# A fixed order for every engine, and the second projection of batches 3 and 4 with still weights, in an attention kernel with a gated long convolution

## The chip, the cores and the metric

The kernel runs on one core of a Trainium2 chip. A core has five engines that run side by side: TensorE (PE) multiplies matrices into PSUM, VectorE (DVE) and ScalarE (ACT) compute on SBUF and PSUM, GpSimd (POOL) computes on SBUF, and SyncE (SP) issues transfers. Sixteen DMA engines move the data that SP, ACT and POOL ask for. Each engine works through its own list of instructions in order and waits on semaphores for the others.

The metric is the time of one execution on the device in microseconds. Before the change it was 381.19 us, the median of three runs (380.57 to 384.06).

## What is computed

Attention over 8 batches, 12 heads, 448 positions, head width 64, with one more term in the denominator, and then a gated convolution over the positions, with the heads joined to a width of 768:

```python
scores = scale * np.matmul(q, k.transpose(0, 1, 3, 2))
m = np.max(scores, axis=-1, keepdims=True)
e = np.exp(scores - m)
attn = e / (np.sum(e, axis=-1, keepdims=True) + np.exp(-m) + 1e-09)
x = np.matmul(attn, v)                       # then (B, S, H * D)
proj = x @ w_proj                            # (768, 2304): x1, x2, x3
X2 = np.fft.rfft(x2, n=S, axis=1)
H = np.fft.rfft(filter_fft, n=S, axis=0)[None, :, :]
x2_conv = np.fft.irfft(X2 * H, n=S, axis=1)
y = x1 * x2_conv * x3
out = y @ w_out
```

Inputs and output are float32; the matrix products are done in bfloat16.

## The kernel before

**Attention.** The work goes by pairs of heads, 6 to a batch, 48 in all; pair i is of batch i // 6. For a pair, the scores are made transposed in four parts: part 0 (lines 825, a remainder of the keys of both heads) and parts 1 to 3 (line 823, 128 keys of each head). ACT takes the exponential of each part (lines 842 and 836). The value products follow, with the remainder first (lines 854 and 862); a column of ones beside v gives the sum. DVE adds 1, takes the reciprocal and multiplies (`norm`, lines 875 to 877). The result `xb` is turned to `xT`, with the channels on the partitions: in batch 0 by PE (line 959), later by DMA transposes on SP (line 950), two for each batch.

**Loads.** In batches 0 and 1 (`staged`) k, q and v come from HBM in float32 (lines 448 and 453, remainders line 465), POOL casts them (lines 475, 481 and 488; for pair 0 it is DVE), and PE turns k and q (lines 514, 516 and 523). From batch 2 on (`loaded`) POOL casts into a buffer `nat` (lines 603, 619, 640, 652), and SP issues DMA transposes into qT and kT (lines 584 and 591), one pair at a time in batch 2 and three pairs at a time later. Weights and the filter come by POOL (lines 717 to 721, 801 and 806).

**The convolution** (`dense`) goes by batch. DVE folds xT into four blocks `xf` by symmetry (lines 1020 to 1028). The second projection, of x2, follows in one of two forms:

- `P` (line 1051): xf is the still operand, the weights move through. 8 groups (4 blocks x 2 halves of the channels) of 6 matmuls of 384 columns. The result has the positions on the partitions, as the next step wants it.
- `PS` (line 1073): the weights are still, xf moves through. 6 groups of 6 matmuls of 452 columns. The result has the channels on the partitions; ACT and DVE copy it in turn into `x2s` (lines 1086 and 1084), and after each three of the six groups SP turns that half with a DMA transpose into `x2` (line 1090).

`TURNED = (5, 6, 7)` names the batches with `PS`. After it come the spectrum (`Z`, lines 1121 and 1125), the products with the filter's spectrum on DVE, the inverse (`I`, line 1210), the unfolding on DVE, and the gates (`G`, line 1171; dt 0 to 5, part 0 and 1, copies at lines 1183 and 1186). Gated y goes through the output projection (`O`, line 987; ACT copies it, line 1285; SP stores it, line 1292). Some of the last projections, all their copies and their stores stand behind a branch (line 1497) that recomputes everything with a maximum where a denominator is too small; with these inputs the branch isn't taken.

**What sets the order.** Each step is added to a planner (`Plan.add`) with its engine, a cost, a wish time, the tokens that it needs and makes, and what it takes and gives back of PSUM banks and buffers. `Plan.run` then goes through time by these costs. At each moment it starts on every free engine the first task, by wish time and among the next 160, that is ready in the plan, and the order in which it started them is the order in which the instructions are written. The planner has a model of the two DMA queues of SP and POOL (delay, landing, shares), gives out PSUM banks (8; score pairs and value products take two each, `hy` tasks, up to five at a time, one each), and from 3 to 36 us fills gaps of PE with small matmuls on a zero tile (line 1438), which keep PE busy. The head starts with 38 such matmuls (`spin`, line 1446). On the chip each engine keeps the written order, and semaphores alone hold it back.

Of the kernel before, what the change touches and what calls it, by code (L numbers as in the profile page):

```python
# [15 lines left out]
BF16 = mybir.dt.bfloat16  # L16
# [4 lines left out]
SP = 112  # L21
NST = S // SP
# [19 lines left out]
class Plan:  # L42
# [11 lines left out]
    LANDING = 1.6  # L54
    DELAY = (1.15, 1.9)
    TURN_ISSUE, TURN_HOLD = 1.4, 0.4
    SHIFT = {}
    OPEN = 8
# [16 lines left out]
    def add(self, eng, cost, want, emit, need=(), make=(), take=(), give=(), dma=0.0, run=256, n=1, after=0.0, begun=(), late=0.0, turn=False, part=None, keep=False, port=False):  # L75
        want += self.SHIFT.get(part, 0.0)
        self.tasks.append((want, len(self.tasks), eng, cost, emit, need, make, take, give, dma, after, run, n, begun, late, turn, keep, port or eng == "POOL" and not dma))

    def run(self):
# [36 lines left out]

        def release():
            h = queues["SP"][0] if queues["SP"] else None
            if h and h[2][1] in begin and h[0] <= clock + 1e-9:
                free["SP"] = max(clock + self.TURN_HOLD, begin.pop(h[2][1]) + self.TURN_ISSUE)  # L120
                heapq.heappush(events, free["SP"])

        def transfers(to):
            nonlocal clock
            while clock < to:
# [7 lines left out]
                step = min([h[1] * total / h[2][11] for h in heads.values()] + [x - clock for x in soon] + [to - clock])  # L133
                clock += step
# [8 lines left out]
        def soonest():  # L143
            heads = [q[0] for q in queues.values() if q and q[0][0] <= clock + 1e-9]
            soon = [q[0][0] for q in queues.values() if q and q[0][0] > clock + 1e-9]
            total = sum(h[2][11] for h in heads)
            return max(min([clock + h[1] * total / h[2][11] for h in heads] + soon), now + 1e-6)
# [25 lines left out]
        def ready(t):  # L173
            e = t[2]
            if t[10] > now + 1e-9:
                return False
# [23 lines left out]
        while any(queue.values()):  # L200
            moved = False
            for e in queue:
                if free[e] > now + 1e-9:
                    continue
                for i, t in enumerate(queue[e][: self.WINDOW]):
# [24 lines left out]
                if t[9]:  # L230
                    q = queues["POOL" if e == "POOL" else "SP"]
                    if t[15]:

                        begin[t[1]], free[e] = now, 1e9
                    q.append([now + self.DELAY[e == "POOL"], t[9], t])
# [54 lines left out]
def kernel(  # L290
# [16 lines left out]
    TURNED = (5, 6, 7)  # L307
# [25 lines left out]
    ld = ctx.enter_context(tc.tile_pool(name="ld", bufs=2))  # L333
# [38 lines left out]
    x2s = nat[:, 0:KNAT].rearrange("p (t a n) -> p t a n", t=NDT, a=4)  # L372
    qn = nat[0:SP, KNAT : 2 * KNAT].rearrange("p (g t c) -> p g t c", g=NHP, t=NST)
# [4 lines left out]
    def stage(g, at, n):  # L378
# [7 lines left out]
            "x2": 1, "x2s": 1, "xs": 2, "t0": 2, "t1": 2, "yh": 1, "g": 1, "x1": 2, "cr": 2, "cw": 1, "cv": 2, "yT": 1, "yR": 1,  # L386
            "os": 3,
        }
    )
    add = plan.add  # L390
# [41 lines left out]
    def staged(b):  # L432
# [3 lines left out]
        for hp in range(NHP):  # L436
# [6 lines left out]
            for n, (name, x, at, size) in enumerate(parts):  # L443
                src = stage(g, at, size)

                def load(name=name, x=x, src=src, hp=hp, g=g):
# [14 lines left out]
                    make=[("s" + name, g)], after=hold, dma=0.92 if name == "q" else 0.7, run=57,  # L461
                    begun=[("i" + name, g)])
                if hp == 0 and name != "q":
# [3 lines left out]
                        dma=1.05, run=57, begun=[("ir", b)])  # L467
# [4 lines left out]
                def cast(name=name, src=src, hp=hp, g=g, eng=eng):  # L472
                    if name == "k":
                        T[g]["kn"] = t = ld.tile([128, 3, 128], BF16, name="k0")
                        eng.tensor_copy(
                            t[:].rearrange("p j (u d) -> p u j d", u=2),
                            src.rearrange("p (u j d) -> p u j d", u=2, j=3),
                        )
                    elif name == "q":
                        T[g]["qn"] = t = ld.tile([SP, NST, 2, DH], BF16, name="q0")  # L480
                        eng.tensor_copy(
                            t[:].rearrange("p j u d -> p u j d"),
# [16 lines left out]
            if hp == 0:  # L499
                for u in range(2):  # L500
# [5 lines left out]
                        need=[("rk", b), "zero ks"] + ([("T", NHP * b - 1)] if b else []), make=[("crk", b)])  # L506
# [68 lines left out]
    def loaded(b):  # L575
# [4 lines left out]
        last = ("S", i0 - NHP - 1, 3)  # L580
# [15 lines left out]

        for n, (name, x) in enumerate((("k", k), ("v", v))):
            add("SP", 0.5, tau(i0) - lead[0] - 0.2 + 0.1 * n,
                lambda name=name, x=x: nc.sync.dma_start(rests[:, "kv".index(name)], shared(x, b)),
                need=[("cr" + name, b - 1)], make=[("r" + name, b)], dma=1.05, run=57)  # L600
        for u in range(2):
# [4 lines left out]
            need=[("rv", b), ("V", i0 - NHP - 1, 1)], make=[("crv", b), ("vr", b)])  # L606

        for hp in range(NHP):
# [8 lines left out]
                need=[("cq", g - QS)] if n >= QS else staged_done, make=[("sq", g)], dma=0.92, run=57)  # L617
# [6 lines left out]
            if hp % few == 0:  # L624
                gs = range(g, g + few)
                add("SP", 1.3, tau(g) - lead[6], lambda hp=hp: q_turn(hp), need=[("cq", i) for i in gs] + [last],
                    make=[("qT", i) for i in gs], dma=(0.65, 1.85)[few > 1], run=11, late=-0.37, turn=few > 1)
            for n, (name, x) in enumerate((("k", k), ("v", v))):
# [3 lines left out]
                room = [("c" + "kv"[old % 2], NHP * NSTAGED + old // 2)] if old >= 0 else staged_done + [  # L632
                    ("T", i) for i in range(NHP * NSTAGED - NHP, NHP * NSTAGED)]
                add("SP", 0.5, tau(g) - lead[0] + 0.1 * n,
                    lambda x=x, hp=hp, src=src: nc.sync.dma_start(src.rearrange("p (u c) -> p u c", u=2), rows(x, b, hp)),
                    need=room, make=[("s" + name, g)], dma=0.7, run=57)
                sv = src.rearrange("p (u j d) -> p u j d", u=2, j=3)
                if name == "k":
# [5 lines left out]
                    if hp % few == 0:  # L644
                        gs = range(g, g + few)
                        add("SP", 1.3, tau(g) - lead[2], lambda hp=hp: k_turn(hp), need=[("ck", i) for i in gs] + [("crk", b), last],
                            make=[("kT", i) for i in gs], dma=(0.95, 1.85)[few > 1], run=11, late=-0.37, turn=few > 1)
                else:
# [5 lines left out]
                    add("POOL", 0.62, tau(g) - lead[3], cast, need=[("sv", g), ("V", g - 2 * NHP, 1)], make=[("cv", g), ("v", g)])  # L654
# [68 lines left out]
    def more_tables():  # L723
# [26 lines left out]
        add("DVE", 1.2, WT, weights, need=["row"], make=["half"], after=WT)  # L750
        add("DVE", 0.35, FT, after=FT, emit=lambda: nc.vector.tensor_scalar(
# [5 lines left out]
        add("DVE", 0.7, BPS, turn_back, need=["bps", "half"], make=["bt"], give=[("hy", "bps")])  # L757
# [3 lines left out]
    def filter_spectrum():  # L761

        def half(par):
            F = W["F"]
            if par == 0:
# [45 lines left out]
    def attention(i):  # L811
# [85 lines left out]
        for t in range(4):  # L897
# [26 lines left out]
            add("ACT", 0.81 if t else 0.44, w - 1.0, lambda t=t: exps(t), need=[("S", i, t)],  # L924
# [624 lines left out]
```

## Time and profile before

| what | value |
|---|---|
| median of three runs | 381.19 us (380.57 to 384.06) |
| the profiled execution's own time | 384.65 us |
| its span, from the first to the last instruction | 382.9 us |
| mean granted TensorE clock | 0.996 |
| PE busy | 365.7 us |
| DVE, ACT, POOL busy | 264.2, 263.5, 109.9 us |
| dummy matmuls in gaps (line 1438), and at the start (line 1446) | 8.8 us, 4.0 us |
| moved by DMA | 66.84 MB, 175 GB/s over the span |

The profile is of one execution, and its durations are those of that execution. In a list of groups, "x576 | 121.8, 352" says that 576 instructions were busy for 121.8 us together and that one took 352 ns on the average. Matmuls overlap in the array, so the durations of single ones add up to more than the busy time; the pace of a run of them is what counts. Idle time of an engine is put down to what ended it, as in "<-DMA qT<-nat". In a list of stretches, DMA is the mean busy share of the 16 engines; their packets overlap, so that it can pass 1.

### The profile page before, as it was taken

Reading aid. Unit: us, or ns where it says so; the run is one execution under the profiler, and the core shown is the slowest. Engines: PE = TensorE matmul, PEld = TensorE weight load, DVE = VectorE, ACT = ScalarE, POOL = GpSimd, SP = SyncE. Lnnn points to the kernel's source line nnn. Section 1 sums busy time; section 2 is a strip of 40 time slices with the busy share of each in tenths; the row PEclk is TensorE's granted clock in tenths of the full one; section 3 lists DMA queues with packets and bytes.
Section 4 is the critical chain, followed back from the end, with each engine's and each line's share of the span. In section 5 each row is a group of like instructions: output and inputs, shape, how many; then the busy total and the mean of one; then the engine's idle time right before and its main releaser. Section 6 shows DMA issues by size and latency. Waiting matters only on the chain. (4 is left out here: it accounts for less than half of the span.)

```text
span 382.9 us, 9530 instructions
## 1 busy us (share of the span) xinstructions
PE 365.7 (96%) x3675; PEld 225.7 (59%) x3675; DVE 264.2 (69%) x677; ACT 263.5 (69%) x457; POOL 109.9 (29%) x240
## 2 busy tenths in 40 slices
PE   8879999999897999999999899999999999999985
PEld 7656666556554576556755565655555556555642
DVE  6377778765799739974499786656586767648650
ACT  5759886776777577777787268887779775444713
POOL 5682716050565242652463443110000000000000
PEclk9989999999999999999999999999999999999999
DMA  8999999996999899999999962493524062323304
GB/s 210 250 231 248 253 220 201 149 225 191 237 251 252 206 242 190 298 233 303 216 230 228 263 181 64 122 192 91 93 35 123 32 121 46 135 64 63 127 4 165
DMA packets 125747, 66.84 MB, mean 175 GB/s; under 512 B 82493, under 2 KB 122112, under 8 KB 125696
## 3 DMA queue, kind: packets, MB, share of 16 engines
q1 hardware_dynamic: 120976, 60.54, 68.2%
q0 software_dynamic: 4480, 5.41, 8.4%
q8 instruction: 29, 0.48, 0.6%
q10 hardware_dynamic: 240, 0.23, 0.2%
q14 instruction: 22, 0.18, 0.1%
HBM read 43.86 MB, written 11.01 MB: 143 GB/s over the span
## 5 line engine op out<-in xcount | busy, mean ns | idle before, releaser
L836 ACT ACTIVATE e<-psum 128x896 bf16<-128x896 f32 x144 | 126.9, 921 | 25.6 <-PE psum L823 25.0
L1171 PE MATMUL psum<-xT,wproj_bf 128*128 128x448 bf16 x576 | 121.8, 352 | 1.7 <-DMA xT<-xb 0.9
L1171 PEld LDWEIGHTS <-wproj_bf 128*128 128x128 bf16 x576 | 54.0, 97 | 47.6 <-issue 4.3
L987 PE MATMUL psum<-wout_bf,yT 128*128 128x384 bf16 x288 | 52.6, 326 | 1.7 <-DVEq L1497 1.7
L1183 ACT CAST x<-psum 128x448 bf16<-128x448 f32 x48 | 25.7, 536 | 28.9 <-PE psum L1171 28.6
L823 PE MATMUL psum<-qT,kT 64*128 64x448 bf16 x288 | 42.4, 358 | 2.9 <-DVE xb L877 2.3
L862 PE MATMUL psum<-vn,e 128*128 128x65 bf16 x1152 | 44.5, 194 | 0.0
L1051 PE MATMUL psum<-wproj_bf,xf 128*113 128x384 bf16 x240 | 43.7, 327 | 0.2
L862 PEld LDWEIGHTS <-e 128*128 128x128 bf16 x1152 | 39.8, 98 | 3.0
L1285 ACT COPY osb<-psum 128x384 f32<-128x384 f32 x56 | 26.4, 488 | 22.1 <-PE psum L987 16.4
L619 POOL CAST nat<-nat 112x512 bf16<-112x512 f32 x36 | 23.8, 666 | 55.0 <-DMA nat<-in_q_dram 51.7
L987 PEld LDWEIGHTS <-yT 128*128 128x128 bf16 x288 | 26.9, 98 | 19.6 <-DVEq L1497 2.0
L1139 DVE TENSOR_TENSOR t<-xs,hrs 113x768 bf16<-113x768 bf16 (+1 forms) x64 | 35.7, 590 | 3.9 <-ACT xs L1133 3.9
L1186 DVE TENSOR_TENSOR g<-x,psum 128x448 bf16<-128x448 bf16 x48 | 29.5, 615 | 11.1 <-PE psum L1171 10.9
L1051 PEld LDWEIGHTS <-xf 128*113 128x113 bf16 x240 | 30.9, 132 | 8.3 <-issue 1.5
L877 DVE TENSOR_TENSOR xb<-psum,den 128x512 bf16<-128x512 f32 x48 | 33.2, 692 | 1.7
L842 ACT ACTIVATE er<-psum 128x448 bf16<-128x448 f32 x48 | 26.5, 552 | 7.6 <-PE psum L825 7.6
L1133 ACT CAST xs<-psum 113x384 bf16<-113x384 f32 (+1 forms) x64 | 28.0, 497 | 4.6 <-PE psum L1121 2.4
L875 DVE TENSOR_SCALAR den<-psum 128x8 f32<-128x8 f32 x48 | 7.8, 162 | 33.2 <-PE psum L862 33.2
L652 POOL CAST vn<-nat 128x192 bf16<-128x192 f32 x58 | 22.5, 414 | 26.5 <-DMA nat<-in_v_dram 15.7
L1219 ACT CAST cr<-psum 128x452 bf16<-128x452 f32 x48 | 25.0, 550 | 5.1 <-PE psum L1210 3.9
L823 PEld LDWEIGHTS <-kT 64*128 64x128 bf16 x288 | 9.4, 94 | 27.7 <-issue 26.3
(125 smaller groups left out, 476.4 us busy)
## 6 DMA issues: line engine op xcount, KB each, us to landing
nat<-in_q_dram SPq DMA_DIRECT2D x47, 224.0 KB, 4.6
out_dram<-osb SPq DMA_DIRECT2D x24, 384.0 KB, 3.3
nat<-in_k_dram SPq DMA_DIRECT2D x41, 192.0 KB, 4.5
nat<-in_v_dram SPq DMA_DIRECT2D x41, 192.0 KB, 4.4
wproj_bf<-in_moe_w_proj_dram POOLq DMA_DIRECT2D x2, 1152.0 KB, 12.8
rests<-in_k_dram SPq DMA_DIRECT2D x8, 192.0 KB, 4.7
rests<-in_v_dram SPq DMA_DIRECT2D x8, 192.0 KB, 4.4
out_dram<-osb SPq DMA_DIRECT2D x8, 192.0 KB, 3.4
```

Source lines behind the costliest of these rows:

```text
L823: nc.tensor.matmul(sc[:, u, 0:S], kT[b % 2][c, hp, t, :], qT[b % 2][c, hp, :])
L836: nc.scalar.activation(to, of, AF.Exp, scale=SCALE)
L842: nc.scalar.activation(to, of, AF.Exp, scale=SCALE)
L862: nc.tensor.matmul(out_bank(u)[:, n, :], P["e"][1 + t][:, u * S + n * 128 : u * S + n * 128 + 128], vn[b % 2][:, hp, 4 * u + t, :], start= ...
L877: nc.vector.tensor_tensor(W["xb", b][:, hp].rearrange("p n (u d) -> p u n d", u=2), op[:, :, :, 0:DH], rec[:].unsqueeze(3).to_broadcast([1 ...
L987: nc.tensor.matmul(ops[:n, :DCH], y[:, dt, 0:n], wout_bf[:, dt, ch * DCH : (ch + 1) * DCH], start=(dt == 0), stop=(dt == NDT - 1),)
L1051: nc.tensor.matmul(pps[:FQ, :DCH], W["xf", b][:, pg, kt, 0:FQ], wproj_bf[:, kt, D + ch * DCH : D + (ch + 1) * DCH], start=(kt == 0), stop= ...
L1133: nc.scalar.copy(L["xs", par, ch][:K, pg % 2, :], L["Z", pg, ch][:K, :DCH])
L1139: nc.vector.tensor_tensor(t[:K], L["xs", par, ch][:K], h, op=ALU.mult)
L1171: nc.tensor.matmul(p[:, :S], wproj_bf[:, kt, 2 * part * D + dt * 128 : 2 * part * D + (dt + 1) * 128], xT()[:, kt, 0:S], start=(kt == 0), ...
L1186: nc.vector.tensor_tensor(g[:, dt, :], L["x1", dt], p[:, :S], op=ALU.mult)
L1285: nc.scalar.copy(L["os", st][:n, ch * DCH : (ch + 1) * DCH], L["O", st, ch][:n, :DCH])
```

## The change

1. **Order.** A tuple `ORDER` gives each of the 2,023 tasks, in the order of `add`, a rank of its own in place of its wish time. With it the planner looks at the first task of each engine's queue only, and no longer at the time before which a task may not start. The plan's run in time still places PSUM banks and dummy matmuls.
2. **The planner's numbers.** Landing, delays and many costs are other ones. A DMA transpose now holds SP in the plan until the transposes ahead of it in the queue are done but for 0.9 us; before, until it came to the front of the queue. All transposes hold SP in this way now. Some needs are written out that the order had given before; the first loads of batch 2 need fewer casts.
3. **Second projection.** `TURNED` takes in batches 3 and 4. Batches 5 to 7 (`WHOLE`) keep their buffer, which lies where k's staging was. Batches 3 and 4 use `x2h`, half as large, so that the second half of the channels waits until the first is turned. It shares its memory with the two-slot buffers of k0 and q0 of batches 0 and 1, which were a tile pool and are now slices of one tile. A memset on DVE clears the part of it that isn't written.

In the new order the engines begin like this (T: turn of a pair; S i,t: scores of pair i, part t; V: value products; ER: remainder of the value products):

- PE: turn of q0, turn of the tables, the 38 dummy matmuls, turn of k0, turn of the k rests, S 0,0, S 0,1, T 1, S 0,2, S 0,3, S 1,1, T 2, S 1,2 with ER 0, ... S 2,3, V 1, S 3,0, S 2,0, T 4, S 3,1, S 3,2 with ER 2, ...
- SP: v2, q1, k rests, v3, k0, k1, v0, v rests, q2, k2, k4, q3, v1, k3, q4, q5, k5, k6, k rests of batch 1, q6, v4, v5, ...
- ACT: load of q0, sines of the tables, a small exponential that loads its table, a small sine, copy of k0, exponentials of pair 0, ...
- POOL, from the casts of pair 4 on: q4, k4, q5, first weight load, k5, v4, second weight load, ...

Around the second projection of the batches 3 and 4 PE has:

- S 27,0, PS 0, S 26,3 and 27,1, PS 1, PS 2, S 27,2 and 27,3 with ER 26, V 26, PS 3, S 28,0, PS 4, G 0,1, PS 5, G 1,0, Z, ...
- S 32,0, G 1,0, PS 2, PS 1, PS 0, S 32,1 and 32,2 with ER 31, V 31, S 33,0 between its halves, PS 3, S 32,3 and 33,1, PS 4, PS 5, Z, ...

and SP has the turns of x2 behind these: "q of pairs 30 to 32 turned, load v38, load v39, first half of batch 3, load q33, xT of batch 4, load q38, load k41, k of pairs 33 to 35 turned, load k38, load v37, second half", and "q of pairs 36 to 38 turned, loads q39, v44, v46, q42, first half of batch 4, loads q41, q44, a store, second half".

```diff
     WINDOW = 160
-    LANDING = 1.6
-    DELAY = (1.15, 1.9)
-    TURN_ISSUE, TURN_HOLD = 1.4, 0.4
+    LANDING = 1.89
+    DELAY = (0.87, 3.1)
+    EARLY = ((3.0, -0.56), (13.0, 0.95))
+    TURN_ROOM = 0.9
     SHIFT = {}
+    ORDER = ()
...
-        want += self.SHIFT.get(part, 0.0)
+        want = self.ORDER[len(self.tasks)] if self.ORDER else want + self.SHIFT.get(part, 0.0)
...
+        def over():
+            return sum(h[1] for h in queues["SP"] if h[2][15]) - self.TURN_ROOM if begin else 0.0
+
         def release():
-            h = queues["SP"][0] if queues["SP"] else None
-            if h and h[2][1] in begin and h[0] <= clock + 1e-9:
-                free["SP"] = max(clock + self.TURN_HOLD, begin.pop(h[2][1]) + self.TURN_ISSUE)
+            if begin and over() <= 1e-9:
+                (i, at), = begin.items()
+                begin.clear()
+                free["SP"] = max(clock, at)
...
-            if t[10] > now + 1e-9:
+            if not self.ORDER and t[10] > now + 1e-9:
                 return False
...
-                for i, t in enumerate(queue[e][: self.WINDOW]):
+                for i, t in enumerate(queue[e][: 1 if self.ORDER else self.WINDOW]):
...
-    TURNED = (5, 6, 7)
+    TURNED = (3, 4, 5, 6, 7)
+    WHOLE = (5, 6, 7)
...
-    ld = ctx.enter_context(tc.tile_pool(name="ld", bufs=2))
...
+    ldm = const.tile([128, 2 * 3 * 128 + 2 * NST * 128], BF16, name="ldm")
+    k0s = [ldm[:, 384 * i : 384 * i + 384].rearrange("p (j c) -> p j c", j=3) for i in range(2)]
+    q0s = [ldm[0:SP, 768 + 512 * i : 768 + 512 * i + 512].rearrange("p (j u d) -> p j u d", j=NST, u=2) for i in range(2)]
+    x2h = ldm[:, 0 : 3 * 4 * 128].rearrange("p (t a n) -> p t a n", t=3, a=4)
...
+    plan.ORDER = (8, 2, 11, 33, 6, 13, 18, 29, 22, 32, 21, 26, 7, 4, 3, 14, 10, 34, 1, 20, 16, 17, 47,
...
-                room = [("c" + "kv"[old % 2], NHP * NSTAGED + old // 2)] if old >= 0 else staged_done + [
-                    ("T", i) for i in range(NHP * NSTAGED - NHP, NHP * NSTAGED)]
+                room = [("c" + "kv"[old % 2], NHP * NSTAGED + old // 2)] if old >= 0 else first[slot]
...
         def still2_back(dt):
-            to, of = x2s[:, dt, :, 0:FQ], L["P", dt]
+            to, of = (x2s[:, dt] if b in WHOLE else x2h[:, dt % 3])[:, :, 0:FQ], L["P", dt]
...
-                x2s[:, ds].rearrange("p t a n -> p (t a n)"),
+                (x2s[:, ds] if b in WHOLE else x2h).rearrange("p t a n -> p (t a n)"),
                 transpose=True,
...
         if b in TURNED and calm:
             for dt in range(NDT):
+                if dt == 3 and b not in WHOLE:
+                    G(0, 0), G(0, 1)
                 PS(dt)
-            G(0, 0), Z(0, 0), G(0, 1), Z(0, 1)
+            if b in WHOLE:
+                G(0, 0), Z(0, 0), G(0, 1), Z(0, 1)
+            else:
+                G(1, 0), Z(0, 0), G(1, 1), Z(1, 0), G(2, 0), Z(0, 1)
...
+        add("DVE", 0.15, tau(NHP * NSTAGED), lambda: nc.vector.memset(x2h[96:128, :, :, FQ:128], 0.0),
+            need=[("T", NHP * NSTAGED - 1), ("T", NHP * NSTAGED - 2)], make=["x2h pads"])
```

More of the change, by code (lines that the diff above doesn't have):

```diff
@@ L133, in transfers @@
                 step = min([h[1] * total / h[2][11] for h in heads.values()] + [x - clock for x in soon] + [to - clock])
+                if over() > 1e-9 and "SP" in heads and heads["SP"][2][15]:
+                    step = min(step, over() * total / heads["SP"][2][11])
                 clock += step
@@ L146, in soonest @@
             total = sum(h[2][11] for h in heads)
+            if over() > 1e-9 and queues["SP"][0] in heads and queues["SP"][0][2][15]:
+                soon = soon + [clock + over() * total / queues["SP"][0][2][11]]
             return max(min([clock + h[1] * total / h[2][11] for h in heads] + soon), now + 1e-6)
@@ L971, in attention @@
         on_act = 4 <= i < 6
-        old = [("G", b - 2)] if b >= 2 else []
+        old = [("G", b - 2)] + [("xf", b - 2, pg) for pg in range(4)] if b >= 2 else []
         if b in XALL or b > 1 and hp < NHP - 1:
```

104 lines of the change are left out of this document (56 added, 48 removed).

## The prediction

> **What bounds the kernel now.** I read the busy times first, then the stretches, then what TensorE (PE) waited for, and last the rows of the operations that the change swaps. The busy times and ten stretches (columns: length; busy time and count of PE, PEld, DVE, ACT, POOL; granted clock; share of the DMA engines; GB/s):
>
> ```profile
> PE 365.7 (96%) x3675; PEld 225.7 (59%) x3675; DVE 264.2 (69%) x677; ACT 263.5 (69%) x457; POOL 109.9 (29%) x240
> ...
> 0.00:10.00 10.00, 8.57 (x105) 7.56 (x106) 6.52 (x27) 5.39 (x8) 5.39 (x18) 1.00 0.87 210
> 10.00:20.00 10.00, 8.76 (x145) 6.21 (x142) 3.37 (x8) 7.46 (x11) 6.10 (x22) 1.00 1.13 252
> 20.00:30.00 10.00, 8.23 (x118) 5.62 (x118) 8.06 (x20) 5.49 (x8) 7.96 (x16) 0.83 1.18 229
> ...
> 100.00:130.00 30.00, 25.92 (x246) 15.09 (x244) 28.22 (x63) 19.84 (x35) 15.89 (x33) 1.00 1.05 221
> 130.00:200.00 70.00, 69.97 (x726) 44.63 (x726) 49.04 (x115) 52.90 (x92) 31.59 (x66) 1.00 1.11 247
> 200.00:220.00 20.00, 18.22 (x145) 10.94 (x143) 16.94 (x44) 10.77 (x19) 8.30 (x16) 1.00 1.11 243
> 220.00:370.00 150.00, 149.94 (x1404) 87.05 (x1403) 102.51 (x274) 103.22 (x184) 10.65 (x22) 1.00 0.40 95
> ```
>
> See that PE has no hole from 130 to 200 us nor from 220 to 370, so only less PE work or fewer holes elsewhere can shorten the kernel. There are three places. (a) The first 40 us: PE is idle for some 5 us, the dummy matmuls that the planner puts into its gaps (line L1438) cover 8.8 us more, and the DMA engines are full. (b) 5.8 us of holes in 100 to 130 and 200 to 220 us. (c) The end, 370 to 382.9, which the change leaves alone: the same 18 matmuls stand ahead of the branch there.
>
> The waits of PE (us in total, times, longest) name the holes:
>
> ```profile
> PE psum L523 <- POOL q L481: 2.7, 3, 1.8
> PE psum L823 <- DVE xb L877: 2.3, 1, 2.3
> PE psum L825 <- DMA qT<-nat: 1.7, 1, 1.7
> ...
> PE psum L1171 <- DMA xT<-xb: 0.9, 1, 0.9
> ...
> PE psum L1171 <- DVE xb L877: 0.8, 1, 0.8
> ```
>
> The first is the head: PE stands in front of a turn whose q is not there. The other four are (b); two of them (1.7 + 0.9) end with a DMA transpose, two (2.3 + 0.8) with a late norm on DVE.
>
> **The second projection, batches 3 and 4.** Groups by form, and two runs in the timeline (start, us):
>
> ```profile
> L1051 PE MATMUL psum<-wproj_bf,xf 128*113 128x384 bf16 x240 | 43.7, 327 | 0.2
> L1073 PE MATMUL psum<-xf,wproj_bf 128*128 128x452 bf16 x108 | 23.4, 357 | 0.0
> ...
> 139.12 2.11 PE L1051 MATMUL psum<-wproj_bf,xf 128*113 128x384 bf16 x12
> 269.88 2.50 PE L1073 MATMUL psum<-xf,wproj_bf 128*128 128x452 bf16 x12
> ```
>
> A run's length less one matmul, over the steps between, is the pace: (2.11 - 0.33)/11 = 0.162 us old, (2.50 - 0.36)/11 = 0.195 us new. A batch goes from 48 x 0.162 = 7.8 to 36 x 0.195 = 7.0 us, so two batches save **1.6 us of PE**, in a stretch without holes, hence off the span. The spectrum step keeps 8 matmuls of 384 columns, at 326 ns in both forms: nothing. The copies out of PSUM go from four each on ACT (480 ns) and DVE (550) to three each (542, 632): 0.3 us less on each, beside PE, nothing.
>
> What comes in is four DMA transposes of half an x2 on SyncE (SP), where DMA runs at 1.11 of its engines, through one half-size buffer. The copy of the fourth output block waits until the first half is turned; until then it holds a PSUM bank, and on DVE the copy of the sixth block, a gate product and the norms stand behind it. Cover: after the third block PE has in the new order one score pair with its rests (0.6), the value matmuls (0.8), two blocks (2.3), a batch 3 gate (1.1) or, in batch 4, a score pair (0.4), a score (0.2) and the last block (1.2): 6.2 us in batch 3, 5.5 in batch 4. Need: copy 0.8, landing, next copy 0.6. Landing after issue, min/median/max, of the x2 turns of now, at 265 us and later where DMA is slack, and then of the kT turns, all through the full stretch:
>
> ```profile
> DMA to landing us min/median/max: 3.6/3.7/4.3
> ...
> DMA to landing us min/median/max: 2.4/4.7/8.4
> ```
>
> At the median the need is 6.1 us, 0.6 over the cover in batch 4; with something for SP's queue ahead of both I take **+1.0**. Bounds: nothing (landing 3.6) and 9.8 - 6.2 + 9.8 - 5.5 = 7.9 us (landing 8.4). The second halves have about 10 us of other work ahead of their readers. [...]
>
> **The head.** I numbered the 2,023 tasks in the order in which they are added (the tuple has as many) and read each engine's new order. SP loads v of pair 2, q1, the k rests and v3 ahead of k0: k0 is its fifth load, not its first. The landings follow each other at the same pace whatever they carry (before: first 4.3 us, fifth 8.0), so k0 lands at about 8.0. PE has the turn of q0 and of the tables ahead of the 38 warm-up matmuls, which took 4.05 us (L1446): q0 cast 5.3, two turns to 6.0, warm-up to 10.0, then k0's turn, its copy (0.46) and the first scores at 11. Before, the first large exponential began at 8.53. On ACT the tables now go sine, exp, sine, exp:
>
> ```profile
> 1.21 1.28 ACT L1451 ACT_TABLE_LOAD   x1 [1.21 <-PEq L1533]
> ```
>
> That is two loads more, 2.6 us; one hides in ACT's wait for k0, the other stands behind k0's copy: first exponential at about 12, 3.5 us later. [...]
>
> Does it reach the end? Pairs 0 to 2 need 12 exponentials, 3 x (3 x 0.81 + 0.44) = 8.6 us, so they end at 20.7 (before 20.1). There both orders meet q4, the 15th load in both, which landed at 20.4. Before, PE waited 1.8 us there, the clock fell (0.83 over 20 to 30 us), and pair 3 went on at 24.2. The new order has a score of pair 3 ahead of that turn, so I put pair 3 at 21.9. From there the rest of pair 3 and pairs 4 and 5 need 3 x 0.81 + 2 x 2.87 = 8.2, the table copies 0.9, one filter copy 0.4: to about 31.5 to 33, against 35.1 before. The second projection of batch 0 began at 41.8; its weights landed at 39.2, and they are second in a queue whose first load is issued as before. So at most 2.6 us are to be had: **-2.0**. Bounds: +3.5 (the late start goes through whole) and -3.5.
>
> **The rest of the order.** Engines keep a fixed order in both kernels; only its content changes. It can take away the 5.8 us of (b). I take half, **-2.9**, as half of it ends with a transpose, whose hold on SP the new plan counts. Bounds: 0, and -5.8; new holes are priced below. The looser conditions of batch 2's loads, at 47 us with DMA full, and a memset of 0.15 us: nothing.
>
> **Sum.** -1.6 + 1.0 - 2.0 - 2.9 = -5.5 us. The profiled execution took 384.65 us (span 382.9 and 1.75 around it), which gives 379.1; it lies 3.5 over the median of the three runs, 381.19, so I forecast 381.2 - 5.5 = **375.7**. Within 1% (377.4 to 385.0) a measurement can hardly tell a change.
>
> **Rivals.**
> - *The transposes of batches 3 and 4 stall PE (slower).* SP is strict, and each of the four stands behind other turns and loads that wait for casts. Price: landings at the worst row 7.9 us, less 1.6, and nothing won elsewhere: 387.5. PE stalls from a landing of 4.8 us in batch 3 and 4.1 in batch 4, and the 1.6 are eaten up at 5.3. For it: kT turns of 131 to 211 us landed after 5.0 to 8.4 us. Against: the gates there can be fed from other banks for a while. A head that passes its 3.5 us on gives 383 with the rest as before, and adds to this. **0.26.**
> - *The order is worth nothing.* Old holes go and others come, the head still hangs on the full DMA queue: 381.2 - 1.6 = 379.6. For it: the five orders were made by a planner before too. **0.14.**
> - *Everything goes.* No hole in (b), the head at its -3.5, no stall: -1.6 - 3.5 - 5.8 gives 370.3. Against: the late first exponential. **0.10.**
> - *The order does not act.* The tuple replaces every wish time and narrows the choice to the head of each queue, so it acts; no chance of its own.
>
> The forecast has 0.50, its own range 372 to 379; a fifth of it lies within 1%. Faster by over 1%: 0.40 + 0.10; within 1%: 0.10 + 0.14; slower: 0.26. The range reaches from 369, under the case in which everything goes, to 388, over the worst landings.
>
> **What would show it.** L1073 180 times and L1051 144 times; PE's busy time without L1438 down by 1.6 us; the first exponential at 12 us, with four table loads on ACT, and batch 0's first L1051 near 39.8; the waits of PE without the 2.3 and 1.7; x2 turns that land 4 to 5 us after issue and no wait of PE behind L1084 or the x2 turn. Wrong if PE has new waits over 1 us between 130 and 220 us, if batch 0's projection starts after 42 us, or if the holes of (b) are only moved.

## The result, and the profile after

| | time | ratio to before, 95% interval |
|---|---|---|
| before | 382.37 us median (380.02 to 387.53, 20 runs) | |
| changed | 379.39 us median (377.22 to 383.84, 20 runs) | 0.9923 [0.9896, 0.9951] |
| profiled execution, changed | 377.33 us, span 375.3 us, clock 0.999 | |

The ratio and its interval are worked out from the runs that lie within 1.5 per cent of the fastest one of their kernel, so they can differ a little from the quotient of the medians.

By the medians the change is worth 3.0 us here, and 5.5 were forecast. The other part of the miss of 3.7 us (379.39 against 375.7) is the starting point: over 20 runs the kernel before has a median of 382.37 us, 1.2 more than the median of the three runs that the forecast started from.

The page of the changed kernel and its stretches (columns as before: length; busy time and count of PE, PEld, DVE, ACT, POOL; granted clock; share of the DMA engines; GB/s):

```profile
PE 358.9 (96%) x3586; PEld 215.8 (58%) x3586; DVE 260.5 (69%) x676; ACT 265.3 (71%) x457; POOL 113.8 (30%) x240
```
```profile
0.00:10.00 10.00, 4.83 (x50) 4.83 (x51) 5.64 (x22) 4.84 (x6) 5.87 (x25) 1.00 0.89 227
10.00:20.00 10.00, 8.91 (x135) 5.97 (x132) 4.71 (x15) 9.33 (x13) 6.45 (x17) 1.00 1.14 270
20.00:30.00 10.00, 9.27 (x156) 6.44 (x153) 8.76 (x21) 9.74 (x14) 7.78 (x15) 1.00 1.14 237
...
100.00:130.00 30.00, 29.71 (x296) 17.41 (x293) 25.00 (x67) 22.19 (x39) 15.41 (x30) 1.00 1.04 226
130.00:200.00 70.00, 67.01 (x664) 39.40 (x665) 50.13 (x118) 49.99 (x88) 30.56 (x63) 1.00 1.09 246
200.00:220.00 20.00, 20.00 (x188) 10.74 (x185) 14.45 (x40) 12.95 (x21) 7.83 (x17) 1.00 0.93 204
220.00:370.00 150.00, 148.19 (x1339) 84.92 (x1338) 99.19 (x266) 99.80 (x183) 9.57 (x18) 1.00 0.47 106
```

Three things are to be seen. From 20 to 30 us ACT is busy for 9.74 us (before 5.49) and the clock stays at 1.00 (before 0.83). From 100 to 130 and 200 to 220 us PE lacks 0.3 us where it lacked 5.9. And from 130 to 200 us, where it lacked nothing, it now lacks 3.0. (The 1.8 us after 220 are the wait at the branch, which stood behind 370 us before.) The waits of PE (us in total, times, longest) give the names:

```profile
PE psum L539 <- DVE ldm L497: 5.2, 1, 5.2
PE psum L1003 <- DVEq L1525: 1.8, 1, 1.8
PE psum L1228 <- DVE g L1204: 1.1, 2, 0.8
PE psum L839 <- DMA kT<-nat: 0.9, 1, 0.9
PE psum L1139 <- DMA x<-ldm: 0.7, 1, 0.7
...
PE psum L1139 <- DVE ldm L1100: 0.5, 2, 0.3
```

The 5.2 us at the start replace dummy matmuls, since the warm-up now stands behind two turns. The next is the branch at the end, which both kernels have. The four after it stand at other places than those of before: a kT turn, the first half x2 turn of batch 3 and what hangs on it, and an inverse that waits for a gate's product on DVE.

The groups by form show the swap of projections as it was meant, and the copies out of PSUM that wait for the half-size buffer:

```profile
L1089 PE MATMUL psum<-xf,wproj_bf 128*128 128x452 bf16 x180 | 38.6, 356 | 0.0
L1067 PE MATMUL psum<-wproj_bf,xf 128*113 128x384 bf16 x144 | 26.6, 328 | 0.0
...
L1100 DVE CAST ldm<-psum 128x452 bf16<-128x452 f32 x6 | 3.7, 631 | 6.8 <-DMA x<-ldm 3.9 <-PE psum L1089 2.9
L1102 ACT CAST ldm<-psum 128x452 bf16<-128x452 f32 x6 | 3.3, 542 | 7.8 <-DMA x<-ldm 4.8 <-PE psum L1089 2.8
```

### One profile is one execution

The two profiles at hand lie 7.3 us apart (384.65 and 377.33 us), but the medians only 3.0. So before anything is put down to the change, each kernel was profiled again. Every profile is accounted for in the same way: the head is the time up to the first matmul of batch 0's second projection, the rest goes from there to the end of PE. Holes are the time of the rest in which no matmul runs. Clock loss is half the length of the records in which the granted clock is 0.5, and work is what remains of the rest.

| profile | head | rest | holes | clock loss in head, in rest | work |
|---|---|---|---|---|---|
| before | 41.78 | 337.04 | 7.98 | 1.71, 0 | 329.06 |
| before_again | 43.20 | 334.36 | 5.24 | 1.71, 0 | 329.12 |
| new_head_old_rest | 39.38 | 335.49 | 5.69 | 0, 0 | 329.80 |
| after | 38.24 | 333.21 | 5.42 | 0, 0 | 327.79 |
| after_again | 39.61 | 335.00 | 6.12 | 0, 1.71 | 327.17 |
| after_more | 38.42 | 339.03 | 9.22 | 0, 1.71 | 328.10 |
| after_third | 39.20 | 334.00 | 5.99 | 0, 0 | 328.01 |
| old_head | 39.41 | 334.66 | 6.10 | 0, 1.71 | 326.86 |
| best1 | 38.92 | 337.04 | 8.60 | 0, 0 | 328.44 |
| best3 | 37.83 | 334.99 | 5.85 | 1.71, 0 | 329.15 |
| best3_twice | 38.05 | 335.43 | 5.92 | 0, 0 | 329.51 |
| best6 | 38.00 | 338.33 | 8.74 | 1.71, 0 | 329.59 |
| best5 | 40.17 | 340.80 | 9.50 | 1.71, 3.41 | 327.89 |
| greedy_layout | 42.52 | 365.39 | 29.07 | 0, 8.53 | 327.79 |

In best3, best3_twice, best6 and best5 the gate G 0,0 (six matmuls, 1.1 us) stands behind the first projection and in all others ahead of it, so there the head lacks it and the work has it.

The four profiles of the changed kernel have a mean head of 38.9 us, the two of before 42.5: **-3.6 us**. The rest has a mean of 335.3 with the new order and of 335.6 with the old one (the first three rows): **-0.3 us**, which is -1.6 of work, +0.4 of holes and +0.9 of clock loss.

### The profile page after: what moved, and what is told of

The parts are those of the page before. It is cut to its first block, busy times and chain, and to the rows that moved or that the text cites. A ratio compares the mean times of both kernels' runs of the same rounds, so it can differ in the third digit from the quotient of the medians.

```text
span 375.3 us, 9304 instructions
## 1 busy us (share of the span) xinstructions
PE 358.9 (96%) x3586; PEld 215.8 (58%) x3586; DVE 260.5 (69%) x676; ACT 265.3 (71%) x457; POOL 113.8 (30%) x240
## 5 line engine op out<-in xcount | busy, mean ns | idle before, releaser
L1189 PEld LDWEIGHTS <-wproj_bf 128*128 128x128 bf16 x576 | 53.2, 97 | 46.4 <-issue 3.4
L878 PE MATMUL psum<-vn,e 128*128 128x65 bf16 x1152 | 46.9, 194 | 0.0
L878 PEld LDWEIGHTS <-e 128*128 128x128 bf16 x1152 | 41.6, 98 | 5.1 <-issue 0.8
L839 PE MATMUL psum<-qT,kT 64*128 64x448 bf16 x288 | 41.5, 355 | 1.4 <-DMA kT<-nat 0.9
L1157 DVE TENSOR_TENSOR t<-xs,hrs 113x768 bf16<-113x768 bf16 (+1 forms) x64 | 39.6, 641 | 4.3 <-ACT xs L1151 4.1
L1089 PE MATMUL psum<-xf,wproj_bf 128*128 128x452 bf16 x180 | 38.6, 356 | 0.0
L1303 ACT COPY osb<-psum 128x384 f32<-128x384 f32 x56 | 25.5, 487 | 18.3 <-PE psum L1003 11.4
L1151 ACT CAST xs<-psum 113x384 bf16<-113x384 f32 (+1 forms) x64 | 29.0, 488 | 12.3 <-PE psum L1139 8.3
L656 POOL CAST nat<-nat 128x384 bf16<-128x384 f32 x29 | 17.1, 594 | 32.5 <-DMA nat<-in_k_dram 31.6
L1067 PE MATMUL psum<-wproj_bf,xf 128*113 128x384 bf16 x144 | 26.6, 328 | 0.0
```

The costliest lines, as they stand in the source:

```text
L839: nc.tensor.matmul(sc[:, u, 0:S], kT[b % 2][c, hp, t, :], qT[b % 2][c, hp, :])
L878: nc.tensor.matmul(out_bank(u)[:, n, :], P["e"][1 + t][:, u * S + n * 128 : u * S + n * 128 + 128], vn[b % 2][:, hp, 4 * u + t, :], start= ...
L1067: nc.tensor.matmul(pps[:FQ, :DCH], W["xf", b][:, pg, kt, 0:FQ], wproj_bf[:, kt, D + ch * DCH : D + (ch + 1) * DCH], start=(kt == 0), stop= ...
L1089: nc.tensor.matmul(pps, wproj_bf[:, kt, D + dt * 128 : D + (dt + 1) * 128], W["xf", b][:, :, kt, 0:FQ], start=(kt == 0), stop=(kt == NDT - 1),
L1151: nc.scalar.copy(L["xs", par, ch][:K, pg % 2, :], L["Z", pg, ch][:K, :DCH])
L1157: nc.vector.tensor_tensor(t[:K], L["xs", par, ch][:K], h, op=ALU.mult)
```

## The experiments

The texts call the kernel as changed "after". Each set was run on one chip with the kernel before beside it. Where a kernel is edited, the tuple of ranks alone is changed, and the diffs show this as lists of tasks. Two edits do more: new_head_old_rest also puts `TURNED` back, and greedy_layout takes the tuple out.

### Both kernels again

> The kernel before once more, unchanged, for a second profile. The two first profiles differ by 7.3 us (384.65 to 377.33) where the medians of 20 runs differ by 3.0. Theory A (the holes of one profile are the order's own): TensorE is again idle for about 6.2 us between 42 and 365 us, at the same places (102.9, 124.7, 202.6, 214.1 us). Theory B (the holes change from one execution to the next with the landings of transfers, and the first profile caught a bad one): 2 to 5 us, at other places or of other lengths, and a span of about 380.5.

Measured: 383.42 us. The waits of its PE:

```profile
PE psum L959 <- DVE xb L877: 3.4, 2, 2.5
...
PE psum L823 <- DVE xb L877: 0.5, 1, 0.5
```

> The changed kernel once more, unchanged. Its first profile had the span 375.3 us, 2 us under the median of its runs, with 3.4 us of holes between 42 and 365 us. Theory A: again 3.4 us of holes at 130.6, 150.7, 155.2 and 182.2 us, and a span of 375 to 376. Theory B: 4 to 7 us of holes, not all at these places, and a span of 376 to 379. In both the first projection of batch 0 starts at 38.2 us if the head depends only on the order, or later if it changes too.

Measured: 380.22 us. The waits of its PE:

```profile
PE psum L839 <- DMA kT<-nat: 2.5, 1, 2.5
...
PE psum L1139 <- DMA x<-ldm: 0.6, 2, 0.4
```

Of the four holes of the kernel before that the forecast wanted to shorten, the 1.7 us (kernel line 825) are gone and the 2.3 us (line 823) are 0.5 here, **in the same kernel, unchanged**. The other two, 0.9 and 0.8 us, are there again with 1.1 and 0.6. The holes of the rest between 42 and 365 us (those of 0.085 us and more) sum to 6.2 us in one execution of before and to 3.7 in the other; in four of the changed kernel to 3.4, 4.3, 7.4 and 4.0. The place is mostly one of a few, but whether it costs 0.4 or 2.5 us differs from one execution to the next. In the first pair of profiles a bad execution of before stood beside a good one of after.

### The changed kernel twice more

> The changed kernel unchanged, timed on the same chip and against the same runs of the kernel before as the next kernel, and with a third profile. So far its ratio is 0.992. Holes of TensorE between 42 and 365 us were 3.4 and 4.3 us in its two profiles, 6.2 and 3.7 in the two of the kernel before. If the holes change from execution to execution, a third value between 3 and 7; the first projection of batch 0 at 38 to 40 us, as soon as its weights have landed.

Measured: 382.65 us median of 12 runs (before 383.37), ratio 0.995 [0.9916, 0.9983]. Its profile is that of an execution of 383.04 us:

```profile
PE psum L1139 <- DMA x<-ldm: 1.7, 1, 1.7
PE psum L839 <- DMA kT<-nat: 1.5, 1, 1.5
```

> The changed kernel as it is, a third time, for comparison within this set. The head's 3.6 us less 0.6 of holes and up to 0.9 of lost clock: ratio 0.992 to 0.995. Profile: batch 0's second projection from 38 to 39.7 us; holes of 3.4 to 7.4 us between 42 and 365 us.

Measured: 380.23 us (before 383.6), ratio 0.994 [0.9904, 0.9977]; the projection of batch 0 at 39.2 us, holes of 4.0 us between 42 and 365. With the first comparison there are three ratios, 0.9923, 0.995 and 0.994, which make the gain 1.9 to 3.0 us. The medians of the three sets differ by 3.0, 0.7 and 3.4 us, so its size is known to a microsecond at best.

### The head and the rest, each alone

Old head with new rest, and new head with old rest. The first 236 ranks are the head; they end just before batch 0's second projection. In the diffs, `before` and `changed` are the tasks in the order in which each kernel issues them.

```diff
 # old_head
-order = changed[:236] + changed[236:]
+order = sorted(changed[:236], key=before.index) + changed[236:]
```

> The changed kernel with its first 236 ranks (everything up to the first matmul of batch 0's second projection) put back into the sequence in which the kernel before has the same tasks; all later ranks as in the changed kernel. If the new head is worth the 3.5 us that the two profiles show (projection of batch 0 from 38.2 instead of 41.8 us), it takes 3.5 us longer than the changed kernel: a ratio to the kernel before of 1.001. If the head is worth nothing, since the later work is held up by the full transfer queue anyway, the ratio stays at 0.992. With the 2.0 us of the forecast, 0.997.

Measured: 384.44 us median (before 383.79), ratio **1.0062** [1.0009, 1.0116]; the medians alone would give 1.0017. Its profile happens to be of its fastest execution (379.76 us), and there the head ends at 39.4 us, so the profile doesn't show what the other runs lost. Their mean granted clocks do: 11 of 12 are below 0.998, and six are at 0.991. One record of 3.41 us at half clock takes 0.0045 off the mean of 380 us (before has one and 0.996), so 0.991 stands for two.

```diff
 # new_head_old_rest
-    TURNED = (3, 4, 5, 6, 7)
+    TURNED = (5, 6, 7)
...
-order = changed
+order = changed[:236] + [t for t in before if t not in changed[:236]]
```

> The head of the changed kernel (its first 236 ranks) with everything behind it as in the kernel before: the old sequence of all later tasks, and batches 3 and 4 with the moving weights (TURNED back to 5, 6, 7, 48 matmuls a batch in place of 36). If the gain of the change is the head's (theory H), the ratio to the kernel before is 0.990 to 0.993, as the whole change's. If the head and the rest share it as forecast (2.0 and 3.5 us of 381), it is 0.995. If the rest gives all, 1.000.

Measured: 381.47 us median (before 383.37), ratio **0.994** [0.9907, 0.9973], beside 0.995 of the changed kernel in the same set. The projection starts at 39.4 us. In the rest its longest hole stands in front of a kT turn, at 134 us, where the two profiles of before have none:

```profile
PE psum L839 <- DMA kT<-nat: 1.8, 1, 1.8
PE psum L1003 <- DVEq L1525: 1.4, 1, 1.4
```

So the head alone brings all that the whole change brings, and the new rest without the new head brings nothing, or takes a little. Still weights in batches 3 and 4 are part of that rest: by the table of profiles their 1.6 us of work are real, and are given back as holes and clock loss. No run has the new order of the rest with moving weights in these batches, so the two parts of the rest were not timed apart.

### The new layout without the order

```diff
-    plan.ORDER = (8, 2, 11, 33, 6, 13, 18, ...)
```

> The changed kernel's layout (transposes of batches 3 and 4, own buffers, still weights in five batches) without the tuple of ranks: the planner goes back to wish times and to its choice among 160 tasks of an engine. Theory A, the searched order is what makes the new layout pay: without it the half x2 turns stand where the wish times put them, holes of 8 us or more between 130 and 260 us, ratio 1.00 to 1.02. Theory B, beyond the head the order makes no difference: ratio 0.995 to 1.003, with the head of before (batch 0's second projection from 41 to 43 us) and holes of 4 to 7 us.

Measured: 413.82 us median, ratio 1.0794 [1.0734, 1.0854]. PE's waits (this kernel's lines are one lower than those of after):

```profile
PE psum L1002 <- DVE yT L1271: 6.4, 5, 1.9
PE psum L1188 <- DMA xT<-xb: 6.0, 3, 3.3
PE psum L840 <- ACT osb L1302: 2.2, 1, 2.2
```

The holes are 29 us and the clock loss 8.5; the work is that of the changed kernel (327.79 us, beside 327.17 to 328.10). Both expectations were too low. The tuple is needed to run this layout at all, but this doesn't price the search: the wish times that remain in the code were written for the old layout, the planner's costs and delays are other ones, and the kernel before, on such wish times, has holes of 5 to 8 us.

### Can the head or the two transposes be made better?

Four orders tried to take away what the profile of after still shows. The first made the table loads and the warm-up early and put k0's load first, with POOL's casts in the order of the loads.

```diff
 # best1
 ACT
-sines, small exp, small sine, copy of k0
+small sine, sines, small exp, copy of k0
 PE
-turn of q0, turn of tables, warm-up, turn of k0
+warm-up, turn of q0, turn of tables, turn of k0
 SP
-v2, q1, k rests, v3, k0, k1
+k0, k rests, q1, k1, v0
```

> The changed kernel with three things in its head undone: the sine table is loaded ahead of its use (two table loads fewer), the 38 warm-up matmuls stand first on TensorE, and k of pair 0 is the first load on SyncE, with the casts on GpSimd in the sequence of the landings. First exponential at 8.5 to 9 us instead of 11.9. If the late start is hidden, as the forecast has it, behind q of pair 4 and the first weights (which landed at 37.9 us, with the projection at 38.2), the ratio to the kernel before stays at 0.992 and the projection of batch 0 starts at 37 to 38.5 us. If ScalarE, busy for 9.3 of each 10 us from 10 to 40 us, sets the pace, the projection starts at 35 to 36 and the ratio is 0.984 to 0.986.

Measured: 385.07 us median of 6 runs (378.94 to 387.35), before 383.79; too few for a ratio. The zero tile that the warm-up reads was still made late on DVE, the warm-up began at 4.9 us, and the first exponential at 11.6. The early start that it was to test didn't happen, so it says nothing on it.

```diff
 # best3
 ACT, PE: as in best1
 DVE
-number, zero, weights, phases, zero tile
+zero tile, number, zero, weights, phases
 POOL
-first weight load, k5, v4, second weight load
+second weight load, first weight load, k5, v4
 PE
-G 0,0, P 2, P 1, P 0, P 3
+P 2, P 1, P 0, P 3, G 0,0
```

> The changed kernel with its warm-up matmuls and the zero tile they need at the very start, the sine table loaded first, the first half of the x2 weights loaded ahead of the x1 weights, and the first gate of batch 0 behind its first four projection groups. The loads on SyncE stay as they are. If the weights' landing sets the start of the projection (37.9 us landed, 38.2 us started), the projection starts when xf of the last channels is folded, at 36.5 to 37.5 us, and the ratio falls by 0.003 to 0.004 from the changed kernel's; first exponential at 9.5 to 10.5 us, as k of pair 0 lands at 7.2. If something else holds it, the start stays at 38 and the ratio at 0.992.

> The kernel of best3 once more, beside best6 on one chip. If its first ratio (0.9925) was its own, 0.990 to 0.995 again, and 1 to 2 us under the changed kernel of the same set. If it was the scatter of executions, 0.994 to 0.998 and level with the changed kernel.

Measured: 380.05 us, ratio 0.9925 [0.9888, 0.9961] (changed kernel in that set 382.65 and 0.995), and 380.93 us, 0.9944 [0.9907, 0.9982] (changed kernel 380.23 and 0.994). Ahead once, level the other time: no gain is shown. What the head says is of more use. The first exponential began at 9.4 us instead of 11.9, and the weights landed at 30.2 and 32.4 in the two profiles instead of 37.9, but the projection began at 37.83 and 38.05 us, against 38.2 to 39.6. Even this lead is not one, since G 0,0 no longer stands ahead: PE was at that place, the start of G 0,0, at 37.11 us in after and 38.18 in after_again. Neither the late exponentials nor the late weights set that point alone; what does stays open. The rest, which best3 does not touch, changes too: from 130 to 200 us PE lacks 0.7 and 1.3 us (3.0 to 5.2 in the changed kernel), and from 100 to 130 us it lacks 1.5 and 1.2 (0.1 to 1.1). So the holes of the rest hang on the head as well.

```diff
 # best6 = best3 and, on SP
-k load of pair 26, v24, v27, turn of k 21 to 23
+turn of k 21 to 23, k load of pair 26, v24, v27
...
-v38, v39, first half x2 turn of batch 3
+first half x2 turn of batch 3, v38, v39
```

> best3 with two transposes issued earlier on SyncE: the kT turn of pairs 21 to 23 ahead of the k load of pair 26, and the first half x2 turn of batch 3 ahead of the v load of pair 38 (the order of the loads and the half x2 turn of batch 4 stay as in the changed kernel). Theory A, the holes of TensorE near 131 to 136 us (0.86, 2.45, 1.50 us in three executions of the changed kernel) and 182 to 187 us (1.2, 0.9, 2.2) are set by the place of these two transposes in SyncE's queue: no hole over 0.5 us at either place, ratio 0.987 to 0.990. Theory B, the stretch is bounded by transfers as a whole and a transpose moved ahead makes the loads behind it late: holes of the same sum elsewhere between 140 and 260 us, ratio 0.992 to 0.997.

Measured: 380.10 us, ratio 0.9902 [0.9866, 0.9937]; the two kernels beside it had 0.9944 and 0.994, and the intervals overlap. Its profile is of an execution near the median, and has the waits:

```profile
PE psum L532 <- POOL ldm L491: 1.9, 1, 1.9
PE psum L1228 <- DVE g L1204: 1.8, 2, 1.6
PE psum L1139 <- DMA x<-ldm: 1.6, 1, 1.6
```

The hole at 131 to 136 us is gone, and the one at 183 is 0.2 us. The DVE copy behind the first half turn waited 1.0 us instead of 3.9. In their place stand 1.6 us up to 152, in front of an inverse that waits for a gate's product, and 1.6 us up to 193.7, for the **second** half turn of the same batch: this was issued 11.7 us after the first, against 9.5 to 10.2 in the four profiles of the changed kernel. The sum between 42 and 365 us is 6.8, more than the 4.0 of after_third. The places are those that theory A names, the sum is what theory B says; the ratio lies between theirs.

```diff
 # best5 = best6 and, on SP, the first loads in the order of the pairs, k0 first, and
-q39, v44, v46, q42, first half x2 turn of batch 4
+first half x2 turn of batch 4, q39, v44, v46, q42
 POOL
-filter load, casts of v0, k2, ... q4
+casts of v0, k2, ... q4, filter load
```

> As best3, and the loads of k, q and v in the sequence of the pairs with k of pair 0 first, the filter's load behind the cast of q of pair 4, and three transposes ahead of the two to four loads that stood before them on SyncE: k of pairs 21 to 23 (TensorE waited 0.9 and 2.5 us for it near 131 us) and the first halves of x2 of batches 3 and 4 (0.7 and 0.4 us near 183 us). If those waits come from SyncE's strict order, they go: 1 to 3 us, and no hole over 0.3 us with a transpose as releaser is left between 125 and 190 us. With the head at 35.5 to 37 us the ratio is 0.983 to 0.988. If the waits come from the full transfer engines, they stay about as long.

Measured: 386.25 us, ratio **1.0058** [1.0023, 1.0092]. PE's waits, and two stretches of it:

```profile
PE psum L1139 <- DMA x<-ldm: 4.3, 1, 4.3
PE psum L870 <- DVE xT L984: 1.9, 1, 1.9
```
```profile
228.00:234.00 6.00, 2.06 (x23) 1.09 (x19) 2.62 (x7) 1.73 (x4) 1.55 (x2) 0.85 0.84 189
234.00:238.00 4.00, 3.62 (x11) 1.65 (x12) 2.12 (x5) 1.31 (x3) 1.42 (x3) 0.50 1.11 262
```

Again the second half comes late: issued at 228.9 us, 9.7 after the first (219.2), where after has 5.9 (216.5 and 222.4). PE stands for 4.3 us, and then runs 6.8 us at half clock, which costs 3.4 more. As in best6, a hole stands at a turn behind those that were moved. This run added three things to best6: the loads, the filter and the third turn. That best6 doesn't have this hole points to that turn, but the others weren't tried alone.

## Why the prediction was right and wrong

| step | forecast | profiles |
|---|---|---|
| less PE work in batches 3 and 4 | -1.6 | -1.6 |
| waits on the half x2 turns | +1.0 | +1.4 in batch 3 (1.2, 0.9, 2.2, 1.2) |
| head | -2.0 | -3.6 |
| the rest of the order | -2.9 | -0.1 (holes of (b) -3.1, other holes +2.1, clock loss +0.9) |
| sum | -5.5 | -3.9; by the timed runs -1.9 to -3.0 |

**PE work: right.** 180 and 144 matmuls at 356 and 328 ns, as forecast, and the rest's work went from a mean of 329.3 to 327.8 us.

**The half x2 turns: right in the wait, near in size by luck.** The line of the x2 turns in batches 3 and 4 of after, with those who waited for it (us, times) and the landings:

```profile
  ACT ldm L1102: 4.8, 1
  DVE ldm L1100: 3.9, 2
...
  PE psum L1139: 0.7, 1
...
DMA to landing us min/median/max: 3.7/4.5/5.6
```

The forecast had PE stall from a landing of 4.8 us in batch 3 and of 4.1 in batch 4. The first half of batch 3 landed after 5.6, 5.2, 5.6 and 5.7 us in the four profiles, and PE stalled in each, for 0.9 to 2.2 us with the short waits behind it: the copies in front of the half-size buffer wait as forecast, and PE stands before the spectrum step. In batch 4 it landed after 3.7, 4.8, 4.4 and 3.8 us, and no hole there was over 0.5; in two of the four profiles batch 4 added 0.6 and 0.3 us in all. The forecast had it the other way round: with one landing of 4.7 us for both batches its 0.6 us came out of batch 4, where PE has less other work, and batch 3 was covered. That 1.0 and 1.4 are close is luck to that extent. The rival that these transposes stall PE for good (387.5 us) asked for landings of 8.4 us, a price of 7.9; none of these came near. The lower bound, nothing, was not met either: PE did wait, and issue to landing took 3.7 to 5.7 us.

**The head: right in sign, too small.** k0 landed at 7.15 us (8.0 forecast), the warm-up ran from 5.9 to 9.9, and the four table loads and the first exponentials came as forecast:

```profile
5.40 1.28 ACT L1479 ACT_TABLE_LOAD   x1
...
6.91 1.28 ACT L1477 ACT_TABLE_LOAD   x1
...
10.65 1.28 ACT L858 ACT_TABLE_LOAD   x1
11.94 0.54 ACT L858 ACTIVATE er<-psum 128x448 bf16<-128x448 f32 x1
12.38 2.53 ACT L852 ACTIVATE e<-psum 128x896 bf16<-128x896 f32 x3
```

The late start is indeed made up at q4: the 12th exponential, the last of pairs 0 to 2, still ends later than before (21.2 us against 20.1), but the 13th starts at 21.1 us against 23.8, and the 24th, the last of pair 5, ends at 31.8 against 35.1. The forecast had 20.7, 21.9 (for which it gives no working) and 31.5 to 33.

The forecast limited the gain to 2.6 us, the time from the landing of the projection's weights (39.2 us) to its start (41.8) in the one profile of before. In before_again these were 38.15 and 43.20, a lag of 5.05. In the changed kernel the weights land hardly earlier on the average (37.9, 39.6, 38.0, 38.9), and the projection starts 0.05 to 0.4 us behind them. So nearly the whole lag goes, 3.8 us on the average of the two profiles of before, and the step was too small mainly because one execution had set its limit. By best3 the landing is not the only thing that holds the projection at this point.

A part of the old lag may be clock. The record at half clock, 3.41 us from 21.8 (before) and 23.5 us (before_again), takes 1.71 us of TensorE's work by itself, and no profile of the changed kernel has one in the head. If it all reached the projection, the -3.6 would be -1.9 of waiting and work, close to the -2.0, and -1.7 of clock. That is not shown: best3 starts its projection at 37.83 us with such a record in the head, and at 38.05 in the profile without one. Counted over the runs: 54 of 81 executions of before, in the three later sets, have a mean clock below 0.998; with the new head and the old rest it is 4 of 12; of the changed kernel 24 of 45, 11 of 12 in the same set as those 4; with the old head and the new rest 11 of 12. The new head takes records at half clock away, and the new rest brings some back.

**The rest of the order: the step that failed.** "It can take away the 5.8 us of (b). I take half, -2.9", with "new holes are priced below"; but only the half x2 turns are given a price, and every other new hole, and the clock behind it, was put at nothing. The holes of (b), from 100 to 130 and 200 to 220 us, are 5.9, 3.3 and 1.5 us in the three profiles with the old rest and 0.3, 0.1, 1.1 and 0.2 in the changed kernel. That is -3.1 on the average, nearly all of a mean of 3.5; that half of one bad execution's 5.8 comes so close to it is luck. From 130 to 200 us, though, PE lacks 3.0, 3.6, 5.2 and 3.4 us where the old rest had 0.0, 0.0 and 1.8. The half x2 turn of batch 3 is 1.4 of this. Of the others, most stand in front of the kT turn of pairs 21 to 23 (0.9, 2.5, 1.5 and 0.9 us), then of an inverse that waits for a gate's product (0.8 and 1.0 in two profiles) and of an xT turn (1.1 in one). A record at half clock follows one of the holes in two of the four profiles. So the new holes outside the half x2 turns and the clock, +2.1 and +0.9, eat up the -3.1. The sign that the forecast gave for this, "new waits over 1 us between 130 and 220 us", is there: 2.45, 1.50, 1.66 and 1.08 us in three of the four profiles. Why they open is known in part only: landings of the kT and x2 turns in the full stretch scatter from 3.7 to 6.9 us, and the hole at the kT turn stands in new_head_old_rest too.

The rival "the order is worth nothing" (379.6) came nearest in its number, but by luck: it had the head as it was and took 1.6 us off 381.2, where 3.0 came off 382.37, and by the runs with the head and the rest apart the gain is the head's.

## What to carry over

Take two or three profiles of the kernel before, and let a hole count as a gain only by what it has on the average: here the holes of one and the same kernel summed to anything from 3.4 to 7.4 us. Where transfers filled a stretch (a DMA share of 1.09 from 130 to 200 us in after), a later transpose came late once others were moved ahead: in best6 the second half turn of batch 3 was issued 11.7 us after the first, against 9.5 to 10.2 in the changed kernel. So the account has to be taken over the whole stretch and not at the place that was mended. And a hole on TensorE is to be priced with the record at half clock that may follow it, which can cost as much as the hole (1.71 us, behind holes of 1.66 to 2.55).

## What the runs showed of the hardware

**Holes of some 2 us are followed by half clock, often but not always (8 of 13).** Three stretches, the first of before and the other two of after_again (behind the hole of 2.45 us that ends at 133.3):

```profile
22.00:26.00 4.00, 3.86 (x48) 2.53 (x49) 2.97 (x7) 2.13 (x3) 4.00 (x9) 0.60 1.22 228
```
```profile
132.00:136.00 4.00, 2.71 (x13) 1.85 (x14) 0.58 (x2) 0.80 (x2) 1.46 (x3) 0.83 1.13 355
136.00:140.00 4.00, 4.00 (x28) 2.66 (x27) 1.10 (x2) 2.40 (x5) 2.76 (x8) 0.75 1.02 298
```

Ahead of the branch the records at half clock are 3.41 us long or twice that, and three times in greedy_layout. In the profiles of all kernels but that one there are 13 holes of 1.6 to 2.6 us ahead of the branch, 8 with such a record at their end or within 2 us behind them (1.66, 1.68, 1.78, 1.88, 1.88, 2.19, 2.45, 2.55) and 5 without (1.74, 1.80, 1.85, 1.90, 2.34). So the length alone doesn't decide: at the same place of best3, 1.68 us had one and, in the other profile, 1.90 had none. What decides it is not shown.

**The landing of one and the same transpose differs from execution to execution.** The kT turn of pairs 21 to 23 landed 5.0, 6.1, 5.4 and 5.7 us after issue in the four profiles of the changed kernel, and PE's hole in front of it was 0.9, 2.5, 1.5 and 0.9 us, in strictly the same order of instructions. The longest landing has the longest hole, but 5.7 us had 0.9 and 5.4 had 1.5, so the landing alone does not set it.
